# A third nested mixing product in layer two, with the attention's normalisation done in layer one's output loop and the gate-weight sums in layer one's attention half

## The chip, the cores and the metric

The kernel runs on one core of a Trainium2 chip. The metric is the time of one execution on the device in microseconds (us), the median over several runs. The core has five engines with instruction streams of their own: TensorE (PE in the profile, with PEld for the loading of weights), VectorE (DVE), ScalarE (ACT), GpSimd (POOL) and SyncE (SP), which issues most of the DMA transfers. Semaphores order them. On-chip memory is SBUF, with 128 partitions; matrix products land in PSUM, here called banks. The profile is one profiled execution.

## The reference

Two layers, each an attention block and a mixer block, over 2048 tokens of 512 features, in float32:

```python
def _A_ref(x, wqkv, wo):                      # 32 heads of 16
    q, k, v = ...                             # x @ wqkv
    phi = lambda t: jnp.where(t > 0, t + 1, jnp.exp(t)) + 1e-6
    pq, pk = phi(q), phi(k)
    kv = jnp.einsum("bhsd,bhse->bhde", pk, v)
    z = jnp.einsum("bhsd->bhd", pk)
    o = einsum(pq, kv) / (einsum(pq, z) + 1e-6)
    return o @ wo
def _B_ref(x, w_in, w_sp, b_sp, w_out):       # Fh = 896
    z = _gelu(x @ w_in)
    z1, z2 = z[..., :Fh], _layernorm(z[..., Fh:])
    g = einsum("ts,bsf->btf", w_sp, z2) + b_sp
    return (z1 * g) @ w_out
for layer in (1, 2):                          # the same weights in both
    x = x + _A_ref(_layernorm(x), wqkv, wo)
    x = x + _B_ref(_layernorm(x), w_in, w_sp, b_sp, w_out)
```

The mixing over tokens, `w_sp` (2048x2048) times z2 (2048x896), is the largest product.

## The kernel before

**Precision.** A float32 product is made as three products of fp32r values: each operand is split into a high part (`high`, line 105, a ScalarE copy that rounds) and a low part (`low`, line 108, a VectorE subtraction of the high part from the value), and `mm3` (lines 117 to 121) multiplies high by high, high by low and low by high. So every operand that TensorE reads costs one ScalarE and one VectorE instruction first, and lines 119, 120 and 121 are the matmuls of nearly all stages.

**The stages of a layer.** Tokens are worked in 16 tiles of 128.
- *P1*, the attention's first half, 17 steps `s`. A tile is normalised (`ln_a`: statistics, lines 230 and 232, and three short GpSimd operations, lines 234 to 239; `ln_b`: normalisation on ScalarE, line 245), transposed through DRAM and a VectorE stream transpose (line 296), projected to K and Q, put through phi (lines 363 to 365), K is split (lines 376, 377) and summed on GpSimd (line 382), and the products of K with x (`Gmm`) are summed over tokens. The last DEFER = 6 tiles leave Q to P2, so the later steps hold K alone: 24 matmuls of 128x512. From step 5 on, `side` splits pieces of the weights wo and win2, to be used in P2; in steps 1 to 4 wv is loaded.
- *P2*, the second half, steps `s` again: the attention's division (`a`, `a2`: lines 650 to 659), its transposes (`b`), the projection with the residual (`c`, `c2` line 691), statistics, normalisation and transposes on TensorE (`c3`, `d_high`, `d_low`; line 257), and the mixer's input projection (`e`, 448 columns at a time; `f`). In layer two the part of `f` is itself done with seven products instead of eight and reads sums of win1 halves, `kept`, that an object `Make` (lines 173 to 211) had made and stored to DRAM in layer one's output loop.
- *P4*, the mixing. w_sp and z2 are seen as 2x2 blocks and multiplied by the seven products P1 to P7 of Strassen and Winograd; the order is a row of `ORDERS` (line 1162). An ordinary product has 8 steps `k` of 24 matmuls (`mm`, lines 1389 to 1391). A product named N1 or N2 stands for P1 or P2's place and is itself computed with seven products: 14 steps of 12 matmuls (`nested_mm`, lines 1329 to 1332). Its weight operands are sums of four w_sp blocks, made by an `Inner` object: 16 units, each one addition or subtraction on VectorE, a high and a low part and two stores to DRAM, from where GpSimd's DMA queue fetches them, 1 MB at a time (line 1193). Its token operands are sums made by `token_sums`. `evac` empties the banks of a product into the gate buffers; `gates` multiplies a finished gate tile with its z1 (line 1411, on GpSimd). Layer one has N2 (last in its order); layer two has N1 and N2.
- *The output loop* `o(i)`, 16 tiles: `zsplit` splits the gated tile (line 108, 896 wide), 21 matmuls by w_out, and the residual is added (line 1514) and stored. In layer one, `join` also starts the next layer there: it loads and normalises the first tiles and makes the first transposed ones (`nxt.T`).

**What sets the order.** The order of instructions on each engine is the order in which this program issues them, written out by hand: steps, tick tables (`MIX_UNITS` gives the steps in which weight-sum units run, `wsteps` those of w_out's pieces) and the `if s == ...` lines. An engine never runs ahead of a waiting instruction in its own stream. Pools of SBUF buffers (`pages` of 128x512, `quads` of four times that, `bigs`) give buffers in turn, and an instruction also waits for the last user of the buffer it gets.

## Time and profile before

| | before |
|---|---|
| median of 3 runs | 1369.39 us (1368.76 to 1369.41) |
| span of the profiled execution | 1367.4 us |
| TensorE busy | 1361.1 us, 6129 instructions |
| VectorE busy | 990.2 us, 1471 |
| ScalarE busy | 618.1 us, 978 |
| GpSimd busy | 462.5 us, 537 |
| moved by DMA | 287.02 MB, 210 GB/s on average |
| granted TensorE clock | 1.000 |

A group row reads: line, engine, operation, output from inputs, shape and count, then its busy time and the mean duration of one, then the engine's idle time just before these instructions and who ended it. A timeline row reads: start, duration, engine, line, operation, and in brackets the idle time before it and what released it. Matmuls overlap in the pipeline, so the duration of one is longer than the distance to the next. "DMA share" is the busy share of the 16 DMA engines.

### The profile page before, as it was taken

How to read it: one execution, taken by the hardware profiler on the slowest of the kernel's cores; microseconds unless marked ns; L12 is line 12 of the kernel's file. 1: busy time of each engine (PE TensorE's matmuls, PEld its weight loads, DVE VectorE, ACT ScalarE, POOL GpSimd, SP SyncE). 2: the span in 40 equal slices, each digit the busy share in tenths (PEclk: the TensorE clock that was granted, in tenths of full speed). 3: DMA queues.
4: the chain of work that ended last, by engine and by line, in shares of the span. 5: the costliest groups of instructions: out<-in, count | busy, mean ns of one | idle time of the engine just before them, and what ended most of it. 6: DMA issues, size and time to landing. Idle time of an engine off the chain costs nothing.

```text
span 1367.4 us, 18070 instructions
## 1 busy us (share of the span) xinstructions
PE 1361.1 (100%) x6129; PEld 1141.0 (83%) x6129; DVE 990.2 (72%) x1471; ACT 618.1 (45%) x978; POOL 462.5 (34%) x537
## 2 busy tenths in 40 slices
PE   9999999999999999999999999999999999999998
PEld 7888888888888888888888888888888888888887
DVE  6775888765757789887667758887767578985742
ACT  6675544444443443441356655534454452442410
POOL 3333475433334137524123434543220001133350
PEclk9999999999999999999999999999999999999999
DMA  5542377877788988897944414777366569854452
GB/s 171 177 131 63 116 246 257 263 247 270 256 249 282 309 277 275 267 355 228 314 124 158 138 56 132 227 224 250 115 198 195 176 225 323 308 183 162 171 189 90
DMA packets 168957, 287.02 MB, mean 210 GB/s; under 512 B 14624, under 2 KB 58528, under 8 KB 165792
## 3 DMA queue, kind: packets, MB, share of 16 engines
q1 hardware_dynamic: 161808, 254.27, 57.7%
q0 software_dynamic: 5184, 28.31, 5.7%
q10 hardware_dynamic: 1872, 3.28, 0.6%
q8 instruction: 48, 0.79, 0.2%
q14 instruction: 45, 0.37, 0.1%
HBM read 196.94 MB, written 88.87 MB: 209 GB/s over the span
## 4 chain that ended last, share of the span: by engine, by line
PE 100%; DVE 0%; DVEq 0%; issue 0%
PE bank L121 19%; PE bank L120 19%; PE bank L119 19%; PE bank L1389 10%; PE bank L1390 10%; PE bank L1391 10%; PE bank L1329 3%; PE bank L1332 3%; PE bank L1331 3%; PE bank L840 1%; PE bank L841 1%; PE bank L839 1%; PE bank L257 1%; PE bank L580 1%; PE bank L445 0%; PE bank L476 0%
## 5 line engine op out<-in xcount | busy, mean ns | idle before, releaser
L1389 PE MATMUL bank<-qd,pg 128*128 128x512 f32 x608 | 236.5, 389 | 0.0
L1390 PE MATMUL bank<-qd,pg 128*128 128x512 f32 x608 | 236.5, 389 | 0.0
L1391 PE MATMUL bank<-qd,pg 128*128 128x512 f32 x608 | 236.5, 389 | 0.0
L1253 DVE TENSOR_TENSOR qd<-qd,qd 128x1024 fp32r<-128x1024 f32 x106 | 145.6, 1373 | 79.0 <-ACT qd L1244 78.4
L1244 ACT ACTIVATE qd<-qd 128x1024 fp32r<-128x1024 f32 x106 | 112.1, 1058 | 128.1 <-DVE qd L1253 52.6
L105 ACT ACTIVATE pg<-pg 128x512 fp32r<-128x512 f32 (+1 forms) x141 | 87.0, 620 | 165.7 <-DVE pg L296 49.4
L121 PE MATMUL bank<-qd,pg 128*128 128x512 f32 x380 | 148.4, 391 | 0.0
L234 POOL TENSOR_SCALAR rs<-mv 128x1 f32<-128x1 f32 x95 | 40.8, 430 | 305.1 <-DVE mv L232 304.7
L1050 POOL TENSOR_TENSOR pg<-pg,pg 128x512 f32<-128x512 f32 x64 | 95.9, 1499 | 135.8 <-DMA pg<-in_wsp_dram 106.4
L1391 PEld LDWEIGHTS bank<-qd,pg 128*128 128x128 f32 x608 | 114.1, 188 | 23.9
L1389 PEld LDWEIGHTS bank<-qd,pg 128*128 128x128 f32 x608 | 114.1, 188 | 23.7
L1390 PEld LDWEIGHTS bank<-qd,pg 128*128 128x128 f32 x608 | 114.1, 188 | 23.5
L1411 POOL TENSOR_TENSOR bg<-bg,pg 128x512 f32<-128x512 f32 x56 | 89.3, 1606 | 127.3 <-DMA pg<-z 123.0
L245 ACT ACTIVATE pg<-pg,nb,rs 128x512 f32<-128x512 f32 x63 | 51.1, 812 | 143.1 <-POOL nb L239 127.6
L119 PE MATMUL bank<-qd,pg 128*128 128x512 f32 x284 | 110.7, 390 | 0.0
L120 PE MATMUL bank<-qd,pg 128*128 128x512 f32 x284 | 110.6, 389 | 0.0
L108 DVE TENSOR_TENSOR pg<-pg,pg 128x512 fp32r<-128x512 f32 (+1 forms) x139 | 102.5, 739 | 11.1 <-DMA z<-pg 3.7
L119 PE MATMUL bank<-bg,qd 128*128 128x448 f32 x256 | 94.0, 367 | 0.0
L120 PE MATMUL bank<-bg,qd 128*128 128x448 f32 x256 | 93.6, 366 | 0.0
L121 PE MATMUL bank<-bg,qd 128*128 128x448 f32 x256 | 93.4, 365 | 0.0
L296 DVE STREAM_TRANSPOSE pg<-pg 128x512 f32<-128x512 f32 x79 | 85.4, 1081 | 9.9 <-DMA pg<-xt 3.4
L119 PE MATMUL bank<-wo,qd 128*128 128x512 f32 x224 | 87.1, 389 | 0.0
(192 smaller groups left out, 3053.9 us busy)
## 6 DMA issues: line engine op xcount, KB each, us to landing
qd<-s SPq DMA_DIRECT2D x64, 512.0 KB, 4.0
pg<-in_wsp_dram SPq DMA_DIRECT2D x96, 256.0 KB, 4.6
qd<-n POOLq DMA_DIRECT2D x24, 1024.0 KB, 7.9
qd<-in_wsp_dram SPq DMA_DIRECT2D x42, 512.0 KB, 4.4
s<-pg SPq DMA_DIRECT2D x64, 256.0 KB, 4.2
pg<-x SPq DMA_DIRECT2D x64, 256.0 KB, 3.6
n<-pg SPq DMA_DIRECT2D x60, 256.0 KB, 4.2
pg<-z SPq DMA_DIRECT2D x56, 256.0 KB, 4.1
```

The costliest lines, as they stand in the source:

```text
L105: nc.scalar.activation(h, src, AF.Copy)
L108: nc.vector.tensor_sub(l, src, h.bitcast(F32))
L119: nc.tensor.matmul(out, ah, bh, start=start, stop=False)
L120: nc.tensor.matmul(out, ah, bl, start=False, stop=False)
L121: nc.tensor.matmul(out, al, bh, start=False, stop=stop)
L1050: nc.gpsimd.tensor_tensor(t, a, b, op=OP.add)
L1244: nc.scalar.activation(wh, r, AF.Copy)
L1253: nc.vector.tensor_sub(wl, r, wh.bitcast(F32))
L1389: m(out, h[:, o], w[:, 0, j, :], start=start, stop=False, skip_group_check=True)
L1390: m(out, h[:, o], w[:, 1, j, :], start=False, stop=False, skip_group_check=True)
L1391: m(out, l[:, o], w[:, 0, j, :], start=False, stop=stop, skip_group_check=True)
L1411: nc.gpsimd.tensor_tensor(u, u, z1, op=OP.mult)
```

## The change

1. In layer two the product P4 is computed as a nested product, N4, at the end of the order (`ORDERS`: "P6", "P7", "N1", "N2", "P5", "P3", "N4"). It combines the four z2 quarter sums (`fourth_operand`, two subtractions on VectorE in each step of P5) with sums of w_sp blocks. Its results go into the gates of the token chunks 0 and 1, so these come last, and the output loop of layer two runs tiles 8 to 15 before 0 to 7. P4 of layer two, its steps and its copies out of the banks are gone; six ScalarE copies in N2 and two sums of the bias in P7 take the place of what it left in the buffers.
2. N4's 16 weight-sum units are made in the last steps of layer one's output loop (tiles 12 to 15) and in steps 1 to 12 of layer two's P1, by a new method `staged` that spreads one unit over three calls (sum, high part, low part and stores). Their pages lie in two spare quads (`Views`); wv is therefore loaded at step 15. `side` takes one piece a step there, not two. N1's units use `staged` as well: in layer two's P2, and in the steps 1, 3, ... 15 of the mixing.
3. The layer norm of layer two's attention moves from P1 into layer one's output loop: after `o(i)` the statistics of its output, which is still on the chip, are taken, and in the next iteration ScalarE normalises it and it is stored transposed; P1 of layer two loads that in place of x.
4. `Make`, the win1 sums, moves from layer one's output loop into layer one's P1 (steps 12 to 17) and the first steps of P2; it works in place on two pages.

The core of the diff:

```diff
-MIX_UNITS = (11, 15, 18, 20, 25, 31, 36, 40), (7, 9, 11, 13, 15, 17, 19, 21)
+MIX_UNITS = (11, 15, 18, 20, 25, 31, 36, 40), (1, 3, 5, 7, 9, 11, 13, 15)
+MAKE_AT = 12, 15, 17
...
+class Views:
+
+
+    def __init__(self, pages, *tiles):
+        self.pages = pages
+        self.free_list = deque(t[:, n // 2, n % 2] for n in range(4) for t in tiles)
+        self.held = {}
+
+    def get(self, shape, dtype=F32):
+        if not self.free_list:
+            return self.pages.get(shape, dtype)
+        t = self.free_list.popleft()
+        self.held[id(t)] = t
+        return t
...
         def add(self, g):
-            a, b = self.raw.pop(g)
-            A11, A12, A21, A22 = (r.rearrange("p (c f) -> p c f", f=P)[:, s] for r in (a, b) for s in (slice(0, 2), slice(2, 4)))
-            s, t = pages.get([P, 2, 2, P]), pages.get([P, 2, 2, P])
-            nc.vector.tensor_add(s[:, 0], A21, A22)
-            nc.vector.tensor_sub(s[:, 1], s[:, 0], A11)
-            nc.vector.tensor_sub(t[:, 0], A11, A21)
-            nc.vector.tensor_sub(t[:, 1], A12, s[:, 1])
-            pages.put(a, b)
-            self.sum[g] = s, t
+            b, a = self.raw[g]
+            A11, A12, A21, A22 = (r[:, s] for r in (a, b) for s in (slice(0, 256), slice(256, 512)))
+            nc.vector.tensor_add(A22, A21, A22)
+            nc.vector.tensor_sub(A21, A11, A21)
+            nc.vector.tensor_sub(A11, A22, A11)
+            nc.vector.tensor_sub(A12, A12, A11)
 
         def split(self, g):
-            self.part[g] = []
-            for r in self.sum.pop(g):
-                h, l = pages.get([P, 2, 2, P], F32R), pages.get([P, 2, 2, P], F32R)
-                split(h, l, r)
-                pages.put(r)
-                self.part[g] += [h, l]
+            r = self.raw[g].pop()
+            h = pages.get(PAGE, F32R)
+            split(h, r.bitcast(F32R), r)
+            self.part[g] = h.bitcast(F32), r, h
...
             for g in range(3):
-                at = i - 2 * g
-                if 0 <= at < 5:
-                    (self.fetch, lambda g: None, self.add, self.split, self.store)[at](g)
+                at = i - MAKE_AT[g]
+                if at == 0:
+                    self.fetch(g)
+                elif at == 1:
+                    self.add(g)
+                elif at in (2, 3):
+                    if at == 3:
+                        self.store(g)
+                    self.split(g)
+                elif at == 4:
+                    self.store(g)
...
+        def norm(self, i):
+            if i < 0:
+                return
+            x, y = self.x.pop(i), pages.get(PAGE)
+            normalise(feats(y, True), feats(x, False), self.ms.pop(i))
+            pages.put(x)
+            self.y = y
+
+        def send(self, i):
+            if i < 0:
+                return
+            self.turn.store(i, self.y)
+            self.kept_d[i] = self.turn.d[i]
+            pages.put(self.y)
...
+            own = inner["N4"] if self.L == 1 else None
+            if own is not None:
+                spare = quads.get([P, 2, 2, 512]), quads.get([P, 2, 2, 512])
+                own.home = Views(pages, *spare)
+            else:
+                self.wv = quads.get([P, 4, 512])
+            each = 2 if own is None else 1
             for s in range(1, NT + 2):
-                self.loadx(s + 3)
+                if s == 1 and own is not None:
+                    self.norm(NT - 1)
+                    self.send(NT - 1)
+                self.loadx(s + 3 if own is None else s + 1)
                 self.turn.load(s + 1)
                 turned = 2 <= s < NT and s not in self.turn.by_pe
                 if turned:
@@ -523,6 +583,14 @@
                 if s <= NT:
                     self.xsplit(s - 1)
                     self.K_split(s - 1)
+                if own is None:
+                    self.make.step(s)
+                if own is not None and s <= NT:
+                    own.staged()
+                    if s == NT - 1:
+                        own.home.close()
+                        quads.put(*spare)
+                        self.wv = quads.get([P, 4, 512])
                 if s + 1 < NT and s + 1 in self.turn.by_pe:
                     self.T(s + 1)
                 self.ln_b(s + 2)
@@ -532,14 +600,13 @@
                     self.Gmm(s - 2)
                 if s == NT + 1:
                     self.late_phi()
-                if s <= 4:
-                    c = s - 1
+                for c in (range(4) if s == NT - 1 else ()) if own is not None else range(s - 1, min(s, 4)):
                     nc.sync.dma_start(self.wv[:, c, :], wqkv[c * P:(c + 1) * P, 1024:1536])
-                else:
-                    for _ in range(min(len(side), 1 if s < 6 else 2)):
+                if s > 4:
+                    for _ in range(min(len(side), 1 if s < 6 else each)):
                         side.popleft().piece()
...
-                        if 6 <= s < 13 if self.seven else 14 <= s < 18:
+                        if not self.seven and 14 <= s < 18:
...
-                    elif s in (8, 11):
-                        own.unit()
+                    elif 6 <= s:
+                        own.staged()
...
+                if not self.seven:
+                    self.p1.make.step(NT + 1 + s)
...
+        def staged(self, more=True):
+            self.out()
+            if self.open is not None:
+                m, k, h, t, keep = self.open
+                l = self.part() if keep else t
+                low(l if keep else t.bitcast(F32R), t, h)
+                if m == 4:
+                    self.home.put(self.S2)
+                self.parts = [(m, k, 0, h, True), (m, k, 1, l, True)]
+                self.open = None
+            if self.added is not None:
+                m, k, t, keep = self.added
+                h = self.part()
+                high(h if h.dtype == F32R else h.bitcast(F32R), t)
+                self.open, self.added = (m, k, h, t, keep), None
+            if not (more and self.due):
+                return
+            self.due -= 1
+            k, u = self.todo.popleft()
+            op = nc.vector.tensor_tensor
+            if u == 0:
+                self.S1 = t = self.raw.pop("22")
+                op(t, self.raw["21"], t, op=OP.add)
+            elif u == 1:
+                t = self.raw.pop("21")
+                op(t, self.raw["11"], t, op=OP.subtract)
+            elif u == 2:
+                self.S2 = t = self.raw.pop("11")
+                op(t, self.S1, t, op=OP.subtract)
+                self.home.put(self.S1)
+            else:
+                t = self.raw.pop("12")
+                op(t, t, self.S2, op=OP.subtract)
+            self.added = (1, 3, 2, 4)[u], k, t, u % 2 == 0
...
-        ORDERS = ("P4", "P1", "P6", "P7", "P5", "P3", "N2"), ("P4", "P6", "P7", "N1", "N2", "P5", "P3")
+        ORDERS = ("P4", "P1", "P6", "P7", "P5", "P3", "N2"), ("P6", "P7", "N1", "N2", "P5", "P3", "N4")
...
-        OWN = {"P1": (2, 0), "P2": (2, 4), "P4": (3, 4)}
+        OWN = {"P1": (0, 0), "P2": (0, 4), "P4": (1, 4)}
...
+        def fourth_operand(self, k):
+            a, b = ztile[k], ztile[k + HT]
+            nc.vector.tensor_sub(a[:, self.H1], a[:, self.H2], b[:, self.H1])
+            nc.vector.tensor_sub(a[:, self.H3], b[:, self.H3], a[:, self.H3])
...
+            if p == "N4":
+                for n, out in {"P1": ((1, self.X),), "P6": ((2, self.X),), "P2": ((1, self.Y),), "P5": ((4, self.Y),),
+                               "P7": ((4, self.X),), "P3": ((2, self.Y),), "P4": ((3, self.X),)}[name]:
+                    for i in range(2):
+                        f = i if n % 2 else 2 + i
+                        u = self.unit(n // 3, f)
+                        (V.tensor_add if f == 3 else V.tensor_sub)(u, u, out[i])
+                if name in ("P2", "P3"):
+                    banks.put(*self.Y)
+                elif name == "P4":
+                    banks.put(*self.X)
+                    self.ready.extend((n, f, False) for n in range(2) for f in range(NF))
+                return
...
+                if not self.nest_late:
+                    if g == 0:
+                        own.begin(2, 1)
+                    elif g <= units[-1] + 3:
+                        own.staged(g in units)
...
+                if p == "P5" and not self.nest_late:
+                    self.fourth_operand(k)
...
+                if nxt is not None:
+                    nxt.norm(i - 1)
+                    if i == NT - 1:
+                        nxt.T(1)
+                self.o(self.order[i], nxt)
+                if nxt is not None:
+                    nxt.ms[i] = stats(nxt.x[i], 1)
+                    nxt.send(i - 1)
                 self.zsplit(i + 2)
-                if make is not None:
-                    make.step(i)
...
+            if i >= 14:
+                nxt.loadx(i - 14)
+            if i == 10:
+                inner["N4"].begin(4, 1)
+            elif i >= 12:
+                inner["N4"].staged()
+            if 8 <= i < 12:
+                for _ in range(2):
+                    (nxt.wk if i < 10 else nxt.wq).fetch()
```

174 lines of the change are left out of this document (98 added, 76 removed).

## The prediction

> **What bounds the kernel now.** I read the header and the busy shares of the page first, then the chain that ended last, then the waits of TensorE, then the rows of a timeline for the spacing of its matmuls.
>
> ```profile
> span 1367.4 us, 18070 instructions
> PE 1361.1 (100%) x6129; PEld 1141.0 (83%) x6129; DVE 990.2 (72%) x1471; ACT 618.1 (45%) x978; POOL 462.5 (34%) x537
> PE 100%; DVE 0%; DVEq 0%; issue 0%
> PE bank L445 <- DVE pg L440: 2.4, 1, 2.4
> L1389 PE MATMUL bank<-qd,pg 128*128 128x512 f32 x608 | 236.5, 389 | 0.0
> ```
>
> TensorE is busy for 1361.1 of 1367.4 us; the chain of waits is 100% PE, and the one wait listed is 2.4 us before the first real matmul. VectorE (72%) and the others only matter where they are late. So the time changes by two things: matmuls that go, and moments at which TensorE has to wait, which hardly exist today. The median of the runs, 1369.39 us, is 2.0 us above this execution's span; I make the sum against the span and carry the 2.0 over unchanged.
>
> What a matmul costs is not its 389 ns, as they overlap, but the distance of their starts:
>
> ```profile
> 1039.61 0.39 PE L1389 MATMUL bank<-qd,pg 128*128 128x512 f32 x1
> ...
> 1045.51 0.39 PE L1391 MATMUL bank<-qd,pg 128*128 128x512 f32 x1
> ```
>
> These are the first and the last of 27 in a row: 5.90 us over 26 distances, 0.227 us each.
>
> **What goes: product P4 of layer two.** It is 8 steps of 24 matmuls, 192 (lines 1389 to 1391, 64 each). As a nested product it is 14 steps of 12, 168 (lines 1329, 1331, 1332, 56 each). 24 fewer at 0.227: **-5.44 us**. Nothing else in the matmul count changes. This gain is certain; the question is how much of it the moved work gives back.
>
> **Layer one's attention output (term A).** The sums over win1 leave the output loop of layer one, where VectorE stands idle, and go into layer one's attention. The last of the three pairs falls at the start of its second half: behind the phi of token tile 14 (line 365) the new order puts one low half (the subtraction of line 108, behind a ScalarE high half) and four 128x256 sums, and behind the phi of tile 15 and before the next transpose one more low half each. The stretch today:
>
> ```profile
> 152.00 0.69 DVE L365 SCALAR_TENSOR_TENSOR z_q<-bank,z_q 128x512 f32<-128x512 f32 x1 [1.45 <-ACT z_q L364]
> 152.60 0.68 DVE L691 TENSOR_TENSOR pg<-pg,bank 128x512 f32<-128x512 f32 x1
> 153.20 0.68 DVE L108 TENSOR_TENSOR pg<-bank,pg 128x512 fp32r<-128x512 f32 x1
> 158.07 0.69 DVE L365 SCALAR_TENSOR_TENSOR z_q<-bank,z_q 128x512 f32<-128x512 f32 x1 [0.23 <-ACT z_q L364]
> 158.68 1.11 DVE L296 STREAM_TRANSPOSE pg<-pg 128x512 f32<-128x512 f32 x1
> 162.35 0.63 DVE L108 TENSOR_TENSOR pg<-pg,pg 128x512 fp32r<-128x512 f32 x1
> 164.38 1.09 DVE L296 STREAM_TRANSPOSE pg<-pg 128x512 f32<-128x512 f32 x1 [0.21 <-DMA pg<-qt]
> 152.39 0.58 ACT L105 ACTIVATE pg<-bank 128x512 fp32r<-128x512 f32 x1
> 154.90 0.39 PE L121 MATMUL bank<-qd,pg 128*128 128x512 f32 x1
> 156.07 0.82 ACT L245 ACTIVATE pg<-pg,nb,rs 128x512 f32<-128x512 f32 x1 [2.62 <-POOL nb L239]
> 157.17 0.60 PE L257 MATMUL bank<-ident,pg 128*128 128x128 f32 x4
> 163.03 0.49 PE L121 MATMUL bank<-qd,pg 128*128 128x512 f32 x1
> L188 DVE TENSOR_TENSOR pg<-pg,pg 128x256 f32<-128x256 f32 x3 | 1.3, 417 | 0.0
> ```
>
> VectorE runs without a gap from 152.00 on. The low half that ends at 153.88 is read by the matmul at 154.90: 1.02 us of room. The inserted low half costs a step of 0.61 (the distance 152.00 to 152.60) after its high half on ScalarE (a wait of some 0.4, as it comes behind the phi in program order), and the four sums 4 x 0.35 to 4 x 0.417: 2.4 to 2.7 in all. TensorE would wait 2.5 - 1.0 = 1.5 us. The same delay runs through line 691, the statistics, GpSimd and the normalisation that ends at 156.89, 0.28 before the transposes at 157.17 that need it: together 2.2. At tile 15 a further low half with its wait (0.6 to 1.1) goes ahead of the transpose at 158.68, whose chain ends with the low half of 162.98, 0.05 before the matmul at 163.03: the trace has no room there at all, so that is another 0.6 to 1.1. The last low half delays the next tile's transpose (line 296 at 164.38, behind 0.21 us of idle time) by up to as much, of which later tiles may take a part back. Sum 2.2 (only the first insertion is felt) to 6.5 (each is, and a GpSimd operation stretches two of them as below); I take **+4.5**, a little above the middle, since three chains in a row have under 0.3 us of room.
>
> **The end of layer two's first attention half (term C).** N4's weight sums (16 units, each one add or subtraction, one high half, one low half, two stores) run there, one unit a step, and the loads of wo and win2 are thinned to one piece a step, so that their splits reach into steps 11 to 15. The layer norm's statistics leave this stretch (0.64 + 0.18 on VectorE in a step, its 0.80 on ScalarE).
>
> ```profile
> 779.88 0.69 DVE L365 SCALAR_TENSOR_TENSOR pg<-bank,pg 128x512 f32<-128x512 f32 x1 [1.08 <-ACT pg L364]
> 781.27 0.69 DVE L377 SCALAR_TENSOR_TENSOR pg<-pg,pg 128x512 fp32r<-128x512 f32 x1
> 782.05 1.30 POOL L382 TENSOR_TENSOR pg<-pg,pg 128x512 f32<-128x512 f32 x1 [2.15 <-DVE pg L377]
> 782.82 0.64 DVE L230 BATCH_NORM_STATS2 st<-pg 128x6 f32<-128x512 f32 x1
> 783.49 0.18 DVE L232 BATCH_NORM_AGGREGATE mv<-st 128x2 f32<-128x6 f32 x1
> 783.93 0.39 PE L120 MATMUL bank<-pg,pg 128*128 128x512 f32 x1
> 785.32 0.69 DVE L365 SCALAR_TENSOR_TENSOR pg<-bank,pg 128x512 f32<-128x512 f32 x1 [0.96 <-ACT pg L364]
> 789.11 0.69 DVE L108 TENSOR_TENSOR pg<-pg,z_h 128x512 fp32r<-128x512 f32 x1 [0.70 <-ACT z_h L105]
> L186 DVE TENSOR_TENSOR pg<-pg 128x256 f32<-128x256 f32 x3 | 4.6, 1522 | 0.0
> 630.46 3.35 POOL L1411 TENSOR_TENSOR bg<-bg,pg 128x512 f32<-128x512 f32 x2 [0.53 <-DMA pg<-z]
> 631.15 1.51 DVE L186 TENSOR_TENSOR pg<-pg 128x256 f32<-128x256 f32 x1
> ```
>
> A step is 785.32 - 779.88 = 5.44 us and has 1.0 us of VectorE idle; taking the statistics out makes it 1.8, but 0.70 of that comes back as the wait for the transposed tile's high half, which stands bare in the row at 789.11. Three steps get 3 x 0.61 = 1.83 in (low half, sum, split of a side piece). By itself that is 0.7 us too much a step. Then there is the neighbour: the sums directly follow line 377, and so does GpSimd's 1.30 us addition of line 382. Where a VectorE operation with two SBUF operands starts beside a GpSimd one, the trace has it last to that one's end and longer: line 186 takes 1522 ns where the same shape at line 188 takes 417. Here one of the two sums would last to the end of line 382's 1.30 us or some 0.2 beyond, in place of 0.61: 0.65 to 0.85 more a step. The split of K ends at 781.96 and is read at 783.93: 2.0 us of room. Lateness over three steps 2.1 (without the neighbour) to 4.2 (with it), less 2.0: 0 to 2.2, and up to 3.2 if the two steps after it do not recover. I take **+2.0**.
>
> The Trainium skill (GPSIMD Engine Reference, 8. Key points) says that GpSimd shares its SBUF interfaces with VectorE, with contention for instructions with two SBUF inputs; it speaks against this placing, and lines 186 and 188 agree. Without that rule C would be near 0.3 and the total 1.7 us less.
>
> **The nested product itself (term E).** N4 streams its operands from DRAM: GpSimd's queue fetches 8 more pieces of 1 MB (24 become 32), SP loads the token blocks. The loads bound this stage more than any other.
>
> ```profile
> qd<-n POOLq DMA_DIRECT2D x24, 1024.0 KB, 7.9
> 568.00:607.00 39.00, 39.00 (x174) 32.23 (x173) 34.18 (x57) 15.10 (x28) 10.42 (x12) 1.00 0.94 344
> 1140.40:1156.70 16.30, 16.30 (x74) 13.49 (x73) 13.68 (x27) 3.40 (x8) 3.17 (x6) 1.00 1.06 409
> ```
>
> Layer one's nested product at the end of its mixing moved 344 GB/s over 39.0 us with TensorE busy throughout (the columns are PE, PEld, DVE, ACT, POOL, clock, DMA share, GB/s), and layer two held 409 GB/s over 16.3 us. N4 has 168 x 0.227 = 38.1 us. Its fetches (8 x 1.0 MB) and its share of the other loads are of the size of layer one's, so it should run as that did. What is new beside it is that the gates of chunks 0 and 1 come only after it, so the GpSimd queue is free for the fetches. Bounds: 0, and 2.0 if a fetch lands a quarter of its 7.9 us late; I take **+0.4**, near the layer-one row. The Trainium skill (DMA: Bandwidth & Descriptors, Specifications) gives some 358 GB/s as the limit of HBM for one core: by it the 6.67 MB of the 409 GB/s window would take 18.6 us, 2.3 more; the row at 409 with TensorE full disagrees and decides.
>
> **Layer one's output loop and the join (terms F and B).** Each o step gains the statistics (0.64 + 0.18 on VectorE), the normalisation of the tile before on ScalarE (0.8), three short GpSimd operations and a store; it loses the win1 sums and 16 loads of x2 in the next stage become 16 loads of the stored tiles.
>
> ```profile
> L234 POOL TENSOR_SCALAR rs<-mv 128x1 f32<-128x1 f32 x95 | 40.8, 430 | 305.1 <-DVE mv L232 304.7
> 629.54 0.69 DVE L1514 TENSOR_TENSOR pg<-pg,bank 128x512 f32<-128x512 f32 x1 [3.07 <-PE bank L121]
> 686.66 0.69 DVE L1514 TENSOR_TENSOR pg<-pg,bank 128x512 f32<-128x512 f32 x1 [1.48 <-PE bank L121]
> 687.27 1.08 DVE L296 STREAM_TRANSPOSE pg<-pg 128x512 f32<-128x512 f32 x1
> 689.04 0.69 DVE L108 TENSOR_TENSOR pg<-pg,pg 128x512 fp32r<-128x512 f32 x1 [0.70 <-ACT pg L105]
> 691.22 0.39 PE L119 MATMUL bank<-qd,pg 128*128 128x512 f32 x1
> ```
>
> VectorE waits 3.07 us for the matmuls of a step there, so 0.82 is covered; without that cover it would be 16 x 0.82. GpSimd is nearer its limit with the gates (1.6 us each, two a step) and three new short operations (0.43 for the first kind, line 234) in a step of 21 matmuls, 4.76: 0 to 1, taken **+0.4**. At the join the first transposed tile of layer two ends at 689.73, some 1.5 us ahead of the matmul at 691.22, and 0.82 of statistics plus 1.2 of staged sums can stand before it: 0 to 0.6, taken **+0.3**.
>
> **The rest at nothing.** The fourth operand (two subtractions a P5 step), the sums of the first product's gate bias in P7, the reversed output order, and the weight pieces of wout lie in mixing steps of 24 matmuls, 5.4 us, where VectorE has its idle time; N1's units move to the steps of P6 and P7, of the same kind; the loads of wv come later but are read only after the stage. If that cover failed, a VectorE step of 0.61 each would show.
>
> **The sum:** 1367.4 - 5.44 + 4.5 + 2.0 + 0.4 + 0.4 + 0.3 = 1369.56 of span, with 2.0 around it **1371.5 us**: 2.1 us or 0.15% above the median shown. About 0.2%, 2.7 us, is what a measurement of this kernel can tell from no change.
>
> **The rivals.**
> - *TensorE stays full; faster.* The terms A to F come out near nothing, because the added work meets VectorE early: TensorE falls behind once, and every later chain then has that much more room. With A at its lower 2.2 and the rest 0 it is 1366.1; with nothing at all 1364.0. For it: the idle waits of VectorE in C and F. Against it: the chain at 163.03 has 0.05 us of room. It decides where A + B + C + E + F stays below 2.7. Chance 0.25.
> - *VectorE falls behind for good in both attention halves; clearly slower.* A 6.5, C 3.2, the others 1.5 together: 1369.4 - 5.4 + 11.2 = 1375.2, and 1377 if the next tiles of layer one are late as well. For it: line 186's 1522 ns. It decides where the sum of the terms is above 8.2. Chance 0.20.
> - *N4 is bound by its transfers.* The fetches on GpSimd's queue land late at N4's start and again at each block: a quarter of 7.9 us, 2.0 in place of 0.4, so 1373.1. Against it: TensorE busy 39.00 of 39.00 at 344 GB/s. Chance 0.10, half of it beyond the 0.2%.
> - *The forecast,* with its parts between 1368.5 and 1374: chance 0.45, of which 0.27 lies within 0.2% and 0.18 above.
>
> Faster 0.25, same 0.27 + 0.05 = 0.32, slower 0.18 + 0.20 + 0.05 = 0.43. The range 1365 to 1377 leaves out about one in ten on each side: below it nearly no wait at all, above it both attention halves late throughout.
>
> **What would show it.** In the changed kernel's profile: 24 fewer matmuls of 128x512 and PE's busy time down by 5.4; in the waits of PE, lines of the attention output's projection and of its transposes waiting for VectorE's low halves and for ScalarE's normalisation (the span of these waits, 4.5 us, is A); waits of the K-times-V matmuls for the split of K (C); no wait of the nested matmuls for a fetch beyond 0.4 us. If PE lists no wait but the first 2.4, every term but the first was wrong. What would make the prediction wrong most easily is VectorE finding its place earlier than program order suggests, or a store that is read again too soon.

## The result, and the profile after

The changed kernel takes 1390.58 us (1390.12 to 1390.92) against 1369.4: slower by 1.56%, ratio 1.0156 with a 95% interval of 1.0140 to 1.0171. The prediction was 1371.5 us, 1365 to 1377. The sign that it held likeliest (slower, 0.43) came true; the size is missed by 19 us and lies outside the range.

The header, the busy shares and the chain of the changed kernel's page, and in the second fence the whole list of TensorE's waits (engine, line, whom it waited for: us in total, times, longest):

```profile
span 1388.4 us, 18267 instructions
PE 1366.8 (98%) x6105; PEld 1136.5 (82%) x6105; DVE 1024.5 (74%) x1541; ACT 625.7 (45%) x1004; POOL 468.1 (34%) x539
PE 35%; DVE 6%; issue 2%; ACT 2%; DMA 2%; POOL 1%; SPq 0%; DVEq 0%; POOLq 0%; ACTq 0%
```

```profile
PE bank L145 <- ACT z_h L131: 6.7, 5, 2.4
PE bank L147 <- DVE pg L134: 5.2, 4, 2.3
PE bank L496 <- DVE pg L491: 2.4, 1, 2.4
PE bank L145 <- ACT pg L131: 1.4, 1, 1.4
PE bank L1453 <- DMA qd<-n: 1.2, 1, 1.2
PE bank L527 <- ACT pg L131: 0.6, 1, 0.6
PE bank L146 <- DVE pg L428: 0.2, 1, 0.2
```

TensorE has the forecast 24 matmuls less (6129 to 6105), and yet its busy time is not 5.4 us lower but 5.7 higher, and its waits are 17.7 us in place of 2.4. Both come from the same moments: TensorE waits, and behind a wait its matmuls start further apart than usual for a while ("slow matmuls"). In the timeline, what two successive matmuls have between their starts beyond 0.227 us, the usual distance of 128x512 ones (counted where they start more than 0.32 us apart), added up by stretch:

| stretch of the changed kernel, us | waits | slow matmuls behind them | together | predicted |
|---|---|---|---|---|
| 100 to 140, layer one's P1, last steps | 0.9 | 0.7 | 1.6 | nothing |
| 140 to 300, layer one's P2 (term A) | 5.4 | 2.2 | 7.7 | 4.5 |
| 300 to 690, mixing and output loop (F) | 0 | 0 | 0 | 0.4 |
| 690 to 730, the join (B) | 2.1 | 1.0 | 3.1 | 0.3 |
| 730 to 850, layer two's P1 (C) | 7.0 | 4.7 | 11.6 | 2.0 |
| 850 to 1200 | 0.6 | 0.2 | 0.9 | nothing |
| 1200 to the end, N4 (E) | 1.3 | 0.2 | 1.5 | 0.4 |

Together 26.3 before rounding; the kernel before has 0.4 of this kind behind 100 us. So -5.4 + 25.9 = 20.5 of the 21.0 us between the two spans; 0.5 is not assigned.

**Slow matmuls behind some waits.** TensorE's timeline where the first low half of layer one's P2 is late, and its next wait:

```profile
156.04 0.39 PE L146 MATMUL bank<-qd,pg 128*128 128x512 f32 x1
158.76 0.56 PE L147 MATMUL bank<-qd,pg 128*128 128x512 f32 x1 [2.33 <-DVE pg L134]
159.12 0.63 PE L145 MATMUL bank<-qd,pg 128*128 128x512 f32 x1
159.55 0.63 PE L146 MATMUL bank<-qd,pg 128*128 128x512 f32 x1
...
162.11 0.57 PE L146 MATMUL bank<-qd,pg 128*128 128x512 f32 x1
162.51 0.40 PE L147 MATMUL bank<-qd,pg 128*128 128x512 f32 x1
169.56 0.50 PE L147 MATMUL bank<-qd,pg 128*128 128x512 f32 x1 [0.88 <-DVE pg L134]
```

After 2.33 us of waiting the matmuls start 0.427 us apart, at nearly half the rate, for some 3.4 us; the granted clock is 0.50 from 159.06 to 162.47 us. The same follows the wait of 2.35 us at 790.94 and, a microsecond later, one of about 1.8 at 806.59, but not the one of 1.74 at 180.00. The prediction had no term for it.

The 1.7 us that such a stretch loses are not simply added to the time. The run with later gates (below) has the same layer one up to here, and there the same wait has no slow matmuls behind it; the granted clock is 1.00 from 158 to 163 us:

```profile
159.20 0.50 PE L147 MATMUL bank<-qd,pg 128*128 128x512 f32 x1 [2.34 <-DVE pg L134]
159.54 0.39 PE L145 MATMUL bank<-qd,pg 128*128 128x512 f32 x1
169.99 0.50 PE L147 MATMUL bank<-qd,pg 128*128 128x512 f32 x1 [1.80 <-DVE pg L134]
```

TensorE reaches the next late operand earlier and waits 1.80 us for it in place of 0.88. From the matmul at 156.04 to the one at 200.09 it is 44.05 us in the changed kernel and 44.05 in that run; between the same two matmuls the kernel before takes 36.48. Of the seven runs with part 4 in layer one, six take 44.04 to 44.16 us there, wherever the slow matmuls stand and whether there are any; only in the run with the units behind the transpose, where some also come behind the last of the waits, it is 45.73. So VectorE's lateness sets the length of this stretch, and slow matmuls cost time where no later wait takes them up.

**Term A in the changed kernel.** VectorE from the phi of tile 14 on:

```profile
153.39 0.69 DVE L416 SCALAR_TENSOR_TENSOR z_q<-bank,z_q 128x512 f32<-128x512 f32 x1 [1.44 <-ACT z_q L415]
154.44 1.36 DVE L134 TENSOR_TENSOR pg<-pg,pg 128x512 fp32r<-128x512 f32 x1 [0.35 <-ACT pg L131]
155.72 0.41 DVE L211 TENSOR_TENSOR pg<-pg 128x256 f32<-128x256 f32 x1
...
157.43 0.68 DVE L758 TENSOR_TENSOR pg<-pg,bank 128x512 f32<-128x512 f32 x1
```

It is the picture of the prediction: the wait for the high half is 0.35, four sums follow, and line 758 (line 691 before) starts 4.04 us behind the start of the phi, before it was 0.60. The inserted block is 3.4 us and not 2.4 to 2.7, because the low half at 154.44 runs beside GpSimd's subtraction of 153.96 and lasts 1.36. The same happens at 163.93 (1.37) and 174.36 (1.36); at 163.93 the phi of tile 15 and the transpose behind it start 2.34 us apart, before it was 0.61.

**Term C.** VectorE and GpSimd in one of layer two's P1 steps:

```profile
785.03 0.69 DVE L428 SCALAR_TENSOR_TENSOR pg<-pg,pg 128x512 fp32r<-128x512 f32 x1
785.64 0.68 DVE L134 TENSOR_TENSOR qd<-qd 128x512 fp32r<-128x512 f32 x1
785.86 1.62 POOL L433 TENSOR_TENSOR pg<-pg,pg 128x512 f32<-128x512 f32 x1 [6.81 <-DVE pg L428]
786.24 1.79 DVE L1249 TENSOR_TENSOR qd<-qd,qd 128x512 f32<-128x512 f32 x1
790.92 0.69 DVE L134 TENSOR_TENSOR pg<-pg,z_h 128x512 fp32r<-128x512 f32 x1 [0.70 <-ACT z_h L131]
793.46 0.69 DVE L428 SCALAR_TENSOR_TENSOR pg<-pg,pg 128x512 fp32r<-128x512 f32 x1
823.67 0.69 DVE L428 SCALAR_TENSOR_TENSOR pg<-pg,pg 128x512 fp32r<-128x512 f32 x1
```

The unit's low half starts ahead of GpSimd's addition and lasts 0.68; its sum starts beside it and lasts 1.79. From the split of K at 785.03 to that at 823.67 five steps take 38.6 us; at TensorE's pace of 5.44 they are 27.2. The difference, 11.4 us, is what the table has for C: VectorE sets the pace of the stage. In these 38.6 us it works 32.2, 6.4 a step and so more than 5.44; the rest is mainly two waits for ScalarE in each step (0.70 and about 0.46). The slow matmuls in the table's row are part of the same lateness and not a cost beside it: the run with the last tile's store behind the loads has the half clock once here where the changed kernel has it twice, and takes as long (120.1 us for the matmuls of 730 to 850).

### The profile page after: what moved, and what is told of

It is laid out like the page before. It is cut to its first block, busy times and chain, and to the rows that moved or that the text cites. A ratio compares the mean times of both kernels' runs of the same rounds, so it can differ in the third digit from the quotient of the medians.

```text
span 1388.4 us, 18267 instructions
## 1 busy us (share of the span) xinstructions
PE 1366.8 (98%) x6105; PEld 1136.5 (82%) x6105; DVE 1024.5 (74%) x1541; ACT 625.7 (45%) x1004; POOL 468.1 (34%) x539
## 5 line engine op out<-in xcount | busy, mean ns | idle before, releaser
L1526 PE MATMUL bank<-qd,pg 128*128 128x512 f32 x544 | 211.6, 389 | 0.0
L1527 PE MATMUL bank<-qd,pg 128*128 128x512 f32 x544 | 211.6, 389 | 0.0
L1528 PE MATMUL bank<-qd,pg 128*128 128x512 f32 x544 | 211.6, 389 | 0.0
L131 ACT ACTIVATE pg<-pg 128x512 fp32r<-128x512 f32 (+1 forms) x152 | 93.5, 620 | 161.7 <-DVE pg L326 62.4
L147 PE MATMUL bank<-qd,pg 128*128 128x512 f32 x380 | 151.4, 398 | 5.2 <-DVE pg L134 5.2
L264 POOL TENSOR_SCALAR rs<-mv 128x1 f32<-128x1 f32 x95 | 47.5, 500 | 270.0 <-DVE mv L262 262.3
L134 DVE TENSOR_TENSOR pg<-pg,pg 128x512 fp32r<-128x512 f32 (+1 forms) x149 | 113.8, 764 | 23.4 <-ACT pg L131 16.7
L1526 PEld LDWEIGHTS bank<-qd,pg 128*128 128x128 f32 x544 | 102.1, 188 | 21.3
L1528 PEld LDWEIGHTS bank<-qd,pg 128*128 128x128 f32 x544 | 102.1, 188 | 21.2
L1527 PEld LDWEIGHTS bank<-qd,pg 128*128 128x128 f32 x544 | 102.1, 188 | 21.1
L145 PE MATMUL bank<-qd,pg 128*128 128x512 f32 x284 | 111.8, 394 | 1.5 <-ACT pg L131 1.4
L146 PE MATMUL bank<-qd,pg 128*128 128x512 f32 x284 | 111.3, 392 | 0.0
L147 PEld LDWEIGHTS bank<-qd,pg 128*128 128x128 f32 x380 | 72.4, 190 | 26.7 <-DVE pg L134 11.6
```

Of the source, the lines that this page charges most:

```text
L131: nc.scalar.activation(h, src, AF.Copy)
L134: nc.vector.tensor_sub(l, src, h.bitcast(F32))
L145: nc.tensor.matmul(out, ah, bh, start=start, stop=False)
L146: nc.tensor.matmul(out, ah, bl, start=False, stop=False)
L147: nc.tensor.matmul(out, al, bh, start=False, stop=stop)
L1526: m(out, h[:, o], w[:, 0, j, :], start=start, stop=False, skip_group_check=True)
```

## The experiments

Each time stands beside runs of the kernel before on the same chip (medians of 1369.0 to 1369.3 us). The first seven are medians of two executions, up to 2.3 us apart, so what an edit does in one stretch is read from the profile and not from a difference of one or two microseconds in the time.

**The win1 sums back in layer one's output loop.**

```diff
-MAKE_AT = 12, 15, 17
+MAKE_AT = 1, 4, 6
...
-                if own is None:
-                    self.make.step(s)
...
                 self.zsplit(i + 2)
                 if nxt is not None:
+                    nxt.make.step(i)
                     self.join(i, nxt)
```

> The changed kernel with part 4 undone: the win1 sums are made in layer one's output loop again (one operation group after each of the tiles 1 to 10), in their new in-place form. Theory (the inserted VectorE work is late at fixed points and TensorE waits for it, then runs its next matmuls slowly): the waits and slow matmuls that the changed kernel shows between 100 and 300 us, 1.6 + 7.7 us over 0.2 in the kernel before, go, so 1390.6 - 9.1 = 1381.5 us; the output loop, where VectorE still waits some 2.1 us a step, shows no new wait. Rival (the waits come from the larger DMA traffic or from the moved layer norm): nothing there changes, 1389.5 to 1391.5 us.

1384.95 us, ratio 1.0117 (1.0088 to 1.0146). Of the 1.6 + 7.7 us 0.2 is left (the kernel before has 0.1); layer one's P2 is as it was, 36.64 us between the two matmuls above against 36.48. But 3.5 us came back elsewhere, most of it from 600 to 730 us, which now hold 5.9 us in place of 3.1: a w_sp block for a unit lands late beside the sums' loads and stores (VectorE idle 2.1 us at 687, `DMA pg<-in_wsp_dram`), and the first transposes behind it are late too. The cause of A is shown; that the output loop had room for the sums without a price was wrong.

**The win1 sums in the attention, in the kernel before** (part 4 alone, in the changed kernel's in-place form).

> The kernel before with part 4 alone: the win1 sums leave the output loop of layer one and go into layer one's attention, in the changed kernel's form and at its steps. Theory (that placing costs by itself what the changed kernel shows between 100 and 300 us): 9.1 us more, 1369.1 + 9.1 = 1378.2 us, with waits of 0.9, 2.5, 1.0 and 1.9 us at the same matmuls and a run of matmuls at 0.427 us behind the second. Rival (it costs that only together with the other parts): within 3 us of 1369.1.

1379.04 us, ratio 1.0071 (1.0051 to 1.0092): 10.0 us more. Three of TensorE's waits in that run:

```profile
PE bank L122 <- DVE pg L109: 5.0, 3, 2.3
PE bank L120 <- ACT z_h L106: 0.8, 1, 0.8
PE bank L1400 <- DVE qd L1263: 0.5, 1, 0.5
```

1.6 us between 100 and 140, 7.7 between 140 and 300. Part 4 costs this by itself, in either kernel.

**Units and side splits behind the stream transpose.**

```diff
                 if turned:
                     self.T_high(s)
+                if own is not None and s <= NT:
+                    own.staged()
...
                 if turned:
                     self.T_low(s)
+                if own is not None and s > 4 and side:
+                    side.popleft().piece()
...
                     self.K_split(s - 1)
...
-                if own is not None and s <= NT:
-                    own.staged()
...
```

> The changed kernel, in layer two's first attention half: the step of a weight-sum unit and the split of a side piece no longer stand directly behind the split of K, where GpSimd's addition runs, but between the stream transpose and the low half of the transposed tile, and behind that low half. No work is left out. Theory (two of VectorE's operations a step last 1.78 us in place of 0.68 beside GpSimd's addition, and the wait of 0.70 us for the transposed tile's high half stands bare): the step falls from 7.2 to 8.4 us to below 6, the waits from 730 to 850 us fall from 11.6 to between 0 and 3 us, 1379 to 1382 us. Rival (VectorE has simply too much to do there, wherever it stands): under 3 us gained, above 1387.5 us. Rival (the loads of the stored tiles are late): no change within 1 us.

1384.87 us, ratio 1.0116 (1.0087 to 1.0146). From 730 to 860 us TensorE has no wait and no slow matmul: the 11.6 us are gone to the last tenth, with the same work. The step:

```profile
776.37 1.30 POOL L433 TENSOR_TENSOR pg<-pg,pg 128x512 f32<-128x512 f32 x1 [6.86 <-DVE pg L428]
776.88 0.69 DVE L416 SCALAR_TENSOR_TENSOR z_q<-bank,z_q 128x512 f32<-128x512 f32 x1 [0.64 <-ACT z_q L415]
777.48 1.08 DVE L326 STREAM_TRANSPOSE pg<-pg 128x512 f32<-128x512 f32 x1
778.41 0.67 DVE L134 TENSOR_TENSOR qd<-qd 128x512 fp32r<-128x512 f32 x1
779.00 0.67 DVE L1251 TENSOR_TENSOR qd<-qd,qd 128x512 f32<-128x512 f32 x1
779.59 0.68 DVE L134 TENSOR_TENSOR pg<-pg,z_h 128x512 fp32r<-128x512 f32 x1
```

Beside GpSimd's addition now stands a phi that reads one operand from a bank, 0.69 us as ever, and the beginning of the stream transpose, 1.08 as ever; the unit's two operations fill the 0.70 us in which VectorE waited for the high half, and last 0.67 each. (In the last steps, which have no Q, the transpose stands beside the addition and the unit's first operation lasts 1.05 to 1.12; TensorE does not wait there either.) The edit does two things, it leaves the neighbour and it fills a wait; the next experiment takes the neighbour alone. Only 5.7 of the 11.6 show in the time: the wait at the join grew to 3.1 us with slow matmuls behind it (5.4 in place of 3.1 from 690 to 730), layer one's P2 took 1.7 more in this run for its slow matmuls behind the last wait, N4 0.9, the stretch from 860 to 1200 0.8.

**GpSimd's sum of K left out in layer two.**

```diff
+            elif self.L == 1:
+                pages.put(r)
             else:
                 nc.gpsimd.tensor_tensor(r, self.zacc, r, op=OP.add)
```

> The changed kernel without GpSimd's addition of the K tiles (line 433) in layer two, which leaves the sum of K over tokens out of layer two's attention. Theory (the neighbour on GpSimd costs 1.1 us for one VectorE operation in each step, and beside it the step still has about half a microsecond too much): the long operations of 1.78 us become 0.68, the step of 7.2 to 8.4 us becomes 6.1 to 7.3, and the waits from 730 to 850 us fall from 11.6 to between 2 and 6 us, 1382 to 1385.5 us. Rival (VectorE's own count of operations decides): less than 2 us gained. Rival (the neighbour alone decides): the waits go to under 1 us, 1379.5 us.

1382.88 us, ratio 1.0100 (1.0079 to 1.0120). From 730 to 860 us 1.8 us are left of 11.6, and the unit's sum is short although its place is the old one:

```profile
788.96 0.69 DVE L428 SCALAR_TENSOR_TENSOR pg<-pg,pg 128x512 fp32r<-128x512 f32 x1
789.57 0.69 DVE L134 TENSOR_TENSOR qd<-qd,qd 128x512 f32<-128x512 f32 x1
790.17 0.69 DVE L1254 TENSOR_TENSOR qd<-qd,qd 128x512 f32<-128x512 f32 x1
```

So about 9.8 of C's 11.6 us are the neighbour, and not the count of VectorE's operations; the medians show 7.7 of them. Both rivals of that expectation fall, the first by size and the second because 1.8 us do remain, just under the 2 to 6 of the theory. Counted between the same matmuls, those of 730 to 850 us, it is 120.1 us in the changed kernel, 110.0 here and 107.9 with the units behind the transpose.

**The last tile's store behind the loads,** with one unit moved from tile 14 to 11.

```diff
                     self.norm(NT - 1)
-                    self.send(NT - 1)
                 self.loadx(s + 3 if own is None else s + 1)
                 self.turn.load(s + 1)
+                if s == 1 and own is not None:
+                    self.send(NT - 1)
...
-            elif i >= 12:
+            elif i >= 11 and i != 14:
                 inner["N4"].staged()
```

> The changed kernel, at the join of the layers: the store of the last normalised tile is issued behind the two loads of the first step and not ahead of them, and the unit step at tile 14 is made at tile 11. Theory (SyncE's queue stands behind the store that waits for ScalarE's normalisation, so the third transposed tile lands late and TensorE waits 1.6 us at 716.6): that wait and most of the 3.1 us between 690 and 730 us go, 1388 to 1389 us. Rival (VectorE's statistics and unit steps delay the first transposes): the wait at 716.6 stays, above 1389.8 us.

1389.68 us, ratio 1.0152 (1.0122 to 1.0181). From 690 to 730 us 1.7 us are left of 3.1, and the longest delay there falls from 1.6 to 1.0. The time lies between the ranges of theory and rival. The store and the unit were moved together, so the run does not say what each gave; it fits SyncE's queue as a part of the cause, not the whole. What stands in the queues at the join of the changed kernel:

```profile
706.94 0.82 ACT L275 ACTIVATE pg<-pg,nb,rs 128x512 f32<-128x512 f32 x1 [3.82 <-POOL nb L269]
707.78 0.38 SPq L311 DMA_DIRECT2D xt<-pg  x1
708.91 0.67 SPq L127 DMA_DIRECT2D pg<-xt  x1
714.80 1.08 DVE L326 STREAM_TRANSPOSE pg<-pg 128x512 f32<-128x512 f32 x1 [0.69 <-DMA pg<-xt]
```

ScalarE waits 3.82 us for the last tile's statistics and normalises it ahead of layer two's phi; the store waits for that, and the load of the third transposed tile stands behind the store.

**Another order at the join** (first transposed tile ahead of output tile 14, units at tiles 10 to 13, last tile's normalisation and store behind the first split of K).

```diff
-            elif i >= 12:
+            elif 10 <= i < 14:
                 inner["N4"].staged()
...
-            if i == 14:
-                nxt.T(0)
...
                     self.K_split(s - 1)
+                if s == 1 and own is not None:
+                    self.norm(NT - 1)
+                    self.send(NT - 1)
...
```

> The changed kernel with another order at the join of the layers: the first transposed tile of layer two is made ahead of output tile 14, N4's first four units run at tiles 10 to 13, and the normalisation of the last tile and its store come behind the split of the first K tile. Theory (three things delay layer two's start: the units and statistics ahead of the first transposes on VectorE, ScalarE's wait for the last tile's normalisation ahead of phi, SyncE's wait for its store): the 3.1 us between 690 and 730 us go to under 0.6, 1388 us. Rival (the loads of the transposed tiles are slow because of the DMA traffic): 1.5 us or more of them stay.

The stretch from 690 to 730 us falls from 3.1 to 0.8 us, so the order was the cause and not the transfers; what each of the three moves gave is not separated. The time, 1389.47 us (1.0148, 1.0127 to 1.0168), moved by 1.1 only; in its profile 1.4 us more stand between 850 and 1200 us, in waits of 0.2 to 0.5, and 0.3 before 690.

**No gates in N4's first seven steps.**

```diff
-                if not (self.nest_late and 49 <= g < 57):
+                if not (49 <= g < 57 if self.nest_late else 60 <= g < 67):
                     self.gates(2 if p == "P3" and not self.nest_late else 1)
```

> The changed kernel with no gate operations in the first seven of N4's 14 steps, so that they do not stand ahead of the 1 MB fetches in GpSimd's queue; they come in the seven steps after. Theory (the fetch of 1292 us was issued late because GpSimd first waited 4.5 us for a gate's z1 tile): the wait of 1.2 us at 1300 goes, 1389.0 to 1389.5 us. Rival (the transfers themselves are at their limit, 407 GB/s): the wait stays, 1390.0 to 1391 us.

The changed kernel's GpSimd at that place:

```profile
1290.32 1.29 POOL L1548 TENSOR_TENSOR bg<-bg,pg 128x512 f32<-128x512 f32 x1 [4.52 <-DMA pg<-z]
1291.57 0.59 POOL L1308 DMA_DIRECT2D qd<-n  x1
```

With the gates later N4 has no wait at all (0 of 1.5 us from 1200 to the end), beside 404 GB/s on the transfers, and none in the three runs below that have the same edit; every other run of the changed kernel has 1.1 to 2.3 us there. So the queue decided. The time did not fall and lies in neither range: 1391.13 us, 1.0162 (1.0133 to 1.0192); its profile has 1.6 us of new waits in layer one's nested product, which the edit does not touch, at the fetched operands. Such waits of some tenths come and go between runs (0 to 0.6 us there in the other runs with the same layer one).

**All of it together.** The edits above (win1 sums in the output loop, units behind the transpose, later gates, the join's order):

> The changed kernel with all of it together: win1 sums in layer one's output loop, weight-sum units and side splits behind the stream transpose, no gates in N4's first seven steps, the other order at the join. No work is left out. Theory (the 24 matmuls are gained in full and everything given back came from the places of the moved work): 1369.1 - 5.4 + 0 to 2 = 1363.7 to 1366 us, faster than the kernel before. Rival (the work moves TensorE's waits elsewhere, so that part of them comes back in the output loop or in N4): 1368 to 1373 us.

1369.17 us, ratio 1.0002 (0.9992 to 1.0011): the 21 us are gone, the gain is not there yet, and the time is in the range of the rival. Most of what is left is at the end of layer one's output loop and the join, 5.8 us, in VectorE's timeline:

```profile
678.71 0.69 DVE L1247 TENSOR_TENSOR pg<-pg,pg 128x512 f32<-128x512 f32 x1 [3.88 <-DMA pg<-in_wsp_dram]
697.74 0.69 DVE L134 TENSOR_TENSOR pg<-pg,pg 128x512 fp32r<-128x512 f32 x1 [1.79 <-ACT pg L131]
```

A unit's w_sp block lands late and stops VectorE for 3.9 us, and a transposed tile's high half stands behind a normalisation on ScalarE.

**The join earlier** (loads of w_sp blocks two ahead from tile 7, win1 sums and the first transposed tiles one tile earlier, transposes ahead of the normalisation).

> The run with all parts moved, with three things changed at the end of layer one's output loop: the loads of the first w_sp blocks two ahead and three tiles earlier, the win1 sums one tile earlier, the first two transposed tiles of layer two one tile earlier and ahead of the normalisation on ScalarE. No work is left out. Theory (the 5.8 us of waits and slow matmuls between 680 and 705 us come from a block that landed late, 3.9 us of VectorE idle, and from a transposed tile's high half behind a normalisation on ScalarE): these go to under 1 us, 1369.2 - 5 = 1364 us, 1363.5 to 1365.5. Rival (the output loop is at the limit of its transfers, 334 GB/s with the DMA engines fully busy from 660 to 680 us, so earlier loads only make other ones late): 1367.5 us or more.

1369.09 us, ratio 1.0001 (0.9991 to 1.0010). The late block is gone, but 4.4 us of waits stand between 600 and 730 us: the first transposed tile now stands in the fullest step of the loop (two weight splits and a unit, TensorE waits 1.3 us for the gated tile's split at 688.88), and the last tile's normalisation waits 2.42 us for a page on ScalarE, ahead of the next phi. The time is in the rival's range again. The rival named the transfers; neither wait was for a load of w_sp, but transfers have a part in both: VectorE stands idle for 0.8 us for the first transposed tile's load ahead of that split, and ScalarE's page is one whose store (`DMA n<-pg`) had to land first. The next run keeps the earlier loads of w_sp and has neither wait.

**The join light.**

```diff
-                    if 0 <= i - 13 < 2:
-                        nxt.T(i - 13)
+                    if i >= NT - 2:
+                        nxt.T(i - NT + 2)
                     nxt.norm(i - 1)
...
-                if s == 1 and own is not None:
+                if s == 3 and own is not None:
                     self.norm(NT - 1)
```

> The run before this one, with the two first transposed tiles at output tiles 14 and 15 again, where no unit and no weight split stands beside them, still ahead of the normalisation on ScalarE, and with the last tile's normalisation and store two steps later in layer two. No work is left out. Theory (the waits of 1.5 us at 688.9 and 1.8 + 0.5 us at 708.7 come from a transposed tile in a VectorE step that was full, and from ScalarE waiting 2.4 us for the last tile's normalisation): they go to under 1 us in all, 1369.1 - 3.2 = 1366 us, 1365 to 1367. Rival (the join has too much VectorE work in any order): above 1368.2 us.

1365.26 us, ratio **0.9967** (0.9955 to 0.9980): faster than the kernel before by 0.33%, with all of the work done. Its page, and in the second fence all its waits:

```profile
span 1364.9 us, 18228 instructions
PE 1356.9 (99%) x6105; PEld 1136.2 (83%) x6105; DVE 1008.2 (74%) x1541; ACT 626.2 (46%) x1004; POOL 468.6 (34%) x539
```

```profile
PE bank L496 <- DVE pg L491: 2.4, 1, 2.4
PE bank L1524 <- ACT bg L1576: 1.3, 1, 1.3
PE bank L1453 <- DVE qd L1369: 0.2, 1, 0.2
PE bank L906 <- DVE pg L948: 0.2, 1, 0.2
PE bank L147 <- DVE pg L134: 0.2, 1, 0.2
```

TensorE's busy time is 4.2 below that of the kernel before. In the medians 4.1 of the 5.4 us are gained, against 1369.32 for the kernel before beside it. The profiled execution was the slowest of six (1366.62), with 1.3 us of waiting for an evacuation; the fastest is 1364.24, a gain of 5.1.

## Why the prediction was wrong

- **The 24 matmuls:** right. 6105 matmuls in place of 6129, and the last run shows that 4.1 of the 5.4 us can be had, 5.1 in its fastest execution.
- **Term A, 4.5 in place of 7.7 (9.3 with P1's end):** the mechanism and its places were right, run by run (1.6 and 7.7 us go with the edit undone, and come with it in the kernel before). The size failed at two steps. The inserted block was put at 2.4 to 2.7 us and takes 3.4, and the low half ahead of a transpose at 0.6 to 1.1 and takes 1.7, because low halves beside GpSimd last 1.36; this was named only for the upper end. The slow matmuls (2.2 in the table) are not a third step: without them the waits themselves are longer, 6.4, and the stretch is as long. And P1's last steps were left out of the sum: the four sums at 106 us delay a transpose by 2.7 us, where line 212 lasts 1.39 beside GpSimd, and TensorE waits 0.9 there.
- **Term C, 2.0 in place of 11.6:** this is the step that failed most. It took two ends from the rows, without and with the neighbour (0 and 3.2), and chose between them, although line 186 had decided for the neighbour already. It set the neighbour at 0.65 to 0.85 us; it is 1.79 - 0.68 = 1.1, since GpSimd's addition grows too, from 1.30 to 1.62. And it counted lateness over three steps, less 2.0 us of room, with the later steps recovering; but in those the low half of a side piece stands beside GpSimd in place of the sum, so no step recovers, and the room is used up once while the lateness comes in five steps. Most of the room was gone ahead of them: the five steps from 742.66 to 785.03 take 8.47 us each, against 8.16 with the units behind the transpose. It is a rate: a step of 7.2 to 8.4 us against 5.44.
- **The sentence on the Trainium skill** (GPSIMD Engine Reference, 8. Key points: shared SBUF interfaces, contention with two SBUF inputs) bore out and should have carried more: taken at its word it speaks for every such pair of operations. The run without GpSimd's addition gives it a price here, 9.8 us. The other sentence, 358 GB/s for one core (DMA: Bandwidth & Descriptors, Specifications), does not bind: in the run with later gates N4 ran without a wait beside 404 GB/s.
- **Term B, 0.3 in place of 3.1:** VectorE's part was seen, the queues of ScalarE (a normalisation ahead of phi) and SyncE (a store ahead of a load) were not looked at, though both instructions are in the diff.
- **Term E, 0.4 in place of 1.5:** the statement that the GpSimd queue is free, since the gates of chunks 0 and 1 come later, was wrong: the gates of chunks 2 and 3 stand in it, and one of them waited 4.5 us for its z1 tile ahead of a fetch.
- **Term F, 0.4 in place of 0:** covered, as the row with 3.07 us of idle time said.
- **The range** ended at 1377 because the upper rival added the upper ends of terms that were themselves too short; it lacked a cost that grows with the number of steps.

## What to carry to other kernels

Where an engine is full, look for the step length and not for the room: work put into each step of a stage whose second engine then needs longer than TensorE costs its excess in every step. Put VectorE operations with two SBUF operands where GpSimd is not adding; here the same unit cost 11.6 us behind the split of K and nothing behind a stream transpose, where it also fills a wait of 0.7 us. Slow matmuls behind a wait of TensorE cost time only where no later wait takes them up: nothing here where VectorE was late anyway, 1.7 us behind the last wait.

## What the runs showed of the hardware that was not expected

- After 2.3 us without a matmul, TensorE can run at nearly half its rate (0.427 us between starts in place of 0.227) for about 3.4 us. The same wait of 2.3 us near 159 had such a run behind it in the changed kernel and none in the run with later gates; waits of some 1.8 us had one at some places (806.59, and 697.76 in the first run with all parts moved) and none at others (180.00). The Trainium skill (TensorE: Matmul & The Clock Gate, Part 1) has the clock fall after an idle window of some 3.4 us that runs freely; that it differs from place to place and from run to run would fit such a window, but less idle time than 3.4 us was enough here. What the window counts was not tried.
- VectorE and GpSimd slow each other where both read two operands from SBUF, and the one that starts second is the longer: GpSimd's addition at 785.86, behind the start of VectorE's low half, takes 1.62 us in place of 1.30, and VectorE's sum at 786.24, behind the start of that addition, 1.79 in place of 0.68. GpSimd's subtraction at 153.96, which started first, takes 1.29. A stream transpose is not slowed (1.09 at 114.67, beside GpSimd's addition of 114.39), and neither is a phi that reads a bank (0.69 at 776.88 in the run with the units behind the transpose).
